# Row order of the second spectrum stage: loads that write 128 partitions instead of 64

## Chip, cores and metric

The kernel runs on one core of one Trainium2 chip. The metric is the device time of one execution in microseconds; several runs give a median and the spread. A profiled execution gives the trace from which the views come: engines PE (TensorE matmul), PEld (its weight load), DVE (VectorE), ACT (ScalarE), POOL (GpSimd) and SP (SyncE, which here issues nearly all DMAs).

## What is computed

One block with two branches, each behind a layer norm with a learned scale and shift: a diagonal state-space convolution along the 2048 tokens, then a token-mixing MLP. The convolution is written with FFTs of length 4096 over 448 channels:

```python
h = _layernorm(x, axis=-1) * (1 + ca) + sa
x = x + ga * _A_ref(h, A_log_A_real, A_A_imag, A_C_real, A_C_imag, A_log_dt, A_D_skip)
h = _layernorm(x, axis=-1) * (1 + cb) + sb
x = x + gb * _B_ref(h, B_w1, B_b1, B_w2, B_b2)
...
# in _A_ref
K = 2.0 * jnp.einsum("dn,dnl->dl", C, P).real
Kf = jnp.fft.rfft(K, L2)
Uf = jnp.fft.rfft(u_t, L2)
y = jnp.fft.irfft(Uf * Kf[None, :, :], L2)[:, :, :L]
```

## The kernel before

The kernel computes the FFTs as two stages of matmuls against tables of cosines and sines. 4096 points are split in 64 x 64; the first stage (`n1` to `k1`) handles 32 tokens at a time, the second (`n2` to `k2`) contracts 128 rows: 64 values of `n2` times the two parts `c` (real, imaginary).

The spectrum of the input u goes as follows. `u_rows` (lines 537 to 558) does the first stage: for each group R and g it makes a tile `yt` and stores it with SP into the DRAM tensor `yu_d`, of shape `[o, k, c, R, g, d]` = `[2, 32, 2, 8, 4, 448]` (line 553). The letters o, R and g together number the 64 values of `n2` (n2 = 16 g + 2 R + o), k is the 32 columns `k1`, c the part, d the channel. `u_load(n)` (lines 567 to 571) loads columns 2n and 2n+1 back: a tile `yi` of 128 partitions x 2 columns x 448 channels, in two DMAs. `u_cols(k)` (lines 573 to 600) does the second stage of column k: one matmul `pu` (line 580) of `yi[:, k % 2]` with the table tile `s2`, whose rows must stand in the same order as those of `yi`. ACT (line 589) or DVE (line 587) evicts `pu` to `uo`, and SP stores each pair of columns into `us_d` (line 593). After both columns of pair n, `u_load(n + 4)` reuses the buffer (there are four), and every second pair `s2_load` (line 565) fetches another part of the table `S2`.

The same stretch of the program also makes the convolution's own kernel, in 56 steps s: exponents and phases by matmul (line 627; `halves`, called by `st_exponents` and `st_phase`) from small tables `lex` and `lph`, which SP loads from the DRAM tensors `pars` (lines 613 and 617, upper and lower rows); exp and sin on ACT (lines 650, 683 to 688); products on DVE and POOL (lines 690 to 696); `kg` on PE (line 717). `lex` has four buffers and `lph` three, so a load waits for PE to have read the table four or three groups earlier. `chain(q)` makes the parameters on DVE and POOL and stores them into `pars` (line 396).

Steps 16 to 31 interleave this with `u_cols`: two or three columns a step, and one after each exponential of the window at step 24. At step 32 the pools of this stage close, and the next stage loads `us_d` as `u` (line 782) and the inverse tables `si` (line 789).

The order on PE, ACT, DVE and POOL is written out by hand (a manual schedule). SP's order is left to a scheduler from step 8 on; it places each DMA by when it expects it to be ready. SP issues in its order and waits for what the next DMA needs: the producer's or the last reader's semaphore, and the DMA eight places earlier, since completions are counted on eight semaphores in turn.

Of the kernel before, what the change touches and what calls it, by code (L numbers as in the profile page):

```python
# [22 lines left out]
P = 128  # L23
# [18 lines left out]
def dft_tables():  # L42
    n1 = np.arange(32)
    k1 = np.arange(32)
    n2 = np.arange(64)
    k2 = np.arange(64)
    nn = 4096
    t = {}
    w = 2 * np.pi * np.outer(n1, k1) / 64
    w1 = np.zeros((2, 32, 32))  # L50
    w1[0] = np.cos(w)
    w1[1] = -np.sin(w)
    w1[0, :, 0] = 1
    w1[1, :, 0] = (-1.0) ** n1
    wc = np.zeros((4, 32, 2, 4, 32))
    for g in range(4):
        for c in range(2):
            wc[g, :, c, g, :] = w1[c]
    t["WU"] = np.tile(w1.transpose(1, 2, 0).reshape(32, 64), (4, 1))

    t["WC"] = wc.reshape(P, 2, 2, 2, 32).swapaxes(3, 4).reshape(P, 2 * P)
    s = np.zeros((2, 64, 32, 2, 64))
    i1 = np.zeros((2, 64, 32, 2, 64))
    i2 = np.zeros((2, 64, 32, 2, 64))

    def inverse(rows, cols, k, m, ang):
        a = np.cos(ang) * 2 / nn
        b = np.sin(ang) * 2 / nn
        i1[0, rows, k, m[0]] = a
        i1[1, rows, k, m[0]] = -b  # L70
        i2[1, rows, k, m[0]] = -a
        i2[0, rows, k, m[0]] = -b
        if len(m) > 1:
            i1[0, rows, k, m[1]] = b
            i1[1, rows, k, m[1]] = a
            i2[1, rows, k, m[1]] = -b
            i2[0, rows, k, m[1]] = a

    for k in range(1, 32):
        ang = 2 * np.pi * np.outer(n2, k + 64 * k2) / nn  # L80
        s[0, :, k, 0] = np.cos(ang)
        s[1, :, k, 0] = np.sin(ang)
        s[0, :, k, 1] = -np.sin(ang)
        s[1, :, k, 1] = np.cos(ang)
        inverse(slice(None), None, k, (0, 1), ang.T)


    for q in range(32):
        ang = 2 * np.pi * n2 * (32 + 64 * q) / nn
        s[1, :, 0, 0, q] = np.cos(ang)  # L90
        s[1, :, 0, 1, q] = -np.sin(ang)
        inverse(q, None, 0, (1,), ang)
    for q in range(33, 64):
        ang = 2 * np.pi * n2 * (64 * (q - 32)) / nn
        s[0, :, 0, 0, q] = np.cos(ang)
        s[0, :, 0, 1, q] = -np.sin(ang)
        inverse(q, None, 0, (0,), ang)
    s[0, :, 0, 0, 32] = 1
    s[0, :, 0, 1, 32] = (-1.0) ** n2
    i1[0, 32, 0, 0] = 1 / nn  # L100
    i2[1, 32, 0, 0] = (-1.0) ** n2 / nn
    s2 = s.reshape(P, 32 * P)

    t["S2"] = s.reshape(2, 4, 8, 2, 32 * P).transpose(3, 0, 2, 1, 4).reshape(P, 32 * P)

    one = np.einsum("cnk,cqkm->km", w1, s.reshape(2, 64, 32, P))
    t["SV"] = one[ones_k1()].T

    order = lambda a: a.reshape(P, 32, 2, 2, 2, 16).transpose(0, 1, 5, 2, 4, 3)
    t["I1"] = order(i1)  # L110
    t["I2"] = order(i2)
    ft = np.zeros((32, 2, 2, 32, 2))
    w = 2 * np.pi * np.outer(k1, n1) / 64
    f0 = np.cos(w)
    f1 = -np.sin(w)
    f0[0] = 1
    f1[0] = (-1.0) ** n1
    for h in range(2):
        ft[:, 0, h, :, h] = f0
        ft[:, 1, h, :, h] = f1  # L120
    t["FT"] = ft.reshape(P, 64)
    fl = np.zeros((4, 4, 2, 2, 2 * LAST, 2, 64))
    for r in range(2):
        for g in range(2):
            fl[r, :, g, r, :, g] = t["FT"].reshape(32, 4, 64)[-2 * LAST :].swapaxes(0, 1)
    t["FL"] = fl.reshape(32, 2 * 2 * LAST * P)


    te = np.zeros((3, 64, 16, 32))
    tg = np.zeros((3, 16, 4, 16, 32))  # L130
    n = np.arange(32)
    for d in range(16):
        te[0, 2 * d : 2 * d + 2, d] = 2 * n + 1
        te[2, 2 * d : 2 * d + 2, d] = -n
        tg[0, d, 0:2, d] = 128 * n
        tg[0, d, 2:4, d] = 1
        tg[2, d, 0:2, d] = -64 * n
        tg[2, d, 2:4, d] = 1
    tg = tg.reshape(3, 16, 2, 2, 512).swapaxes(1, 2)
    tt = np.concatenate([te.reshape(3, 64, 512), tg.reshape(3, 64, 512)], 1)  # L140
    tt[1] = -tt[0]
    t["TT"] = tt.reshape(3, P, 512)

    v1, v2 = (t.pop(k).reshape(2, 64, 32, P) for k in ("I1", "I2"))
    j1 = np.stack([v1[0], v2[1]])
    j2 = np.stack([v1[1], v2[0]])
    for nm, tabs, n in (("SI", (s2, v1, v2), NP), ("SJ", (s2, j1, j2), 1), ("SK", (s2, v1), NP)):
        tabs = [a.reshape(P, NP, 2, P)[:, :n] for a in tabs]  # L150
        t[nm] = np.stack(tabs, 2).reshape(P, n * len(tabs) * 2 * P)
    return {k: np.ascontiguousarray(v.astype(np.float32)) for k, v in t.items()}


def ones_k1():

    return [0] + list(range(1, 32, 2))
# [69 lines left out]
def tile_adaln_s4d_mixer(ctx, tc, i, out):  # L227
    nc = tc.nc
# [5 lines left out]
    yu_d = dram.tile([2, 32, 2, 8, 4, D], F32, name="yu_d")  # L234
# [13 lines left out]
    with ExitStack() as es:  # L248
# [309 lines left out]
            dve.append(out)  # L558

        yis, s2s, uos = {}, {}, {}  # L560
        yu_v = yu_d.rearrange("o k c R g d -> o (c R g) k d")

        def s2_load(n):
            s2s[n] = sp2.tile([P, 4, P], F32, tag="s2", name="s2")
# [2 lines left out]
        def u_load(n):  # L567

            yis[n] = up.tile([P, 2, D], F32, tag="yi", name="yi", bufs=4)
            for o in range(2):  # L570
                nc.sync.dma_start(yis[n][64 * o : 64 * o + 64], yu_v[o, :, 2 * n : 2 * n + 2])

        def u_cols(k):
            n, kk = divmod(k, 4)
            if kk % 2 == 0:
                uos[k // 2] = up.tile([P, 2, 2, DC], F32, tag="uo", name="uo", bufs=4), []
            yi, s2 = yis[k // 2], s2s[n]
            uo, done = uos[k // 2]
            pm = pms.tile([P, D], F32, tag="ms", name="pu")
            T.matmul(pm, s2[:, kk], yi[:, k % 2], start=True, stop=True)  # L580

            def out():
                o, chunks = uo[:, :, k % 2], lambda t: t.rearrange("p (c d) -> p c d", c=2)
                if k in ones_k1():

                    j = ones_k1().index(k)
                    stt(o, chunks(mod[0]), svt[:, j : j + 1], chunks(pm), ALU.mult, ALU.add)
                else:
                    S.copy(o, chunks(pm))
                done.append(kk)  # L590
                if len(done) == 2:
                    to = us_d[:, :, k // 2 * 2 : k // 2 * 2 + 2].rearrange("c p k d -> p c (k d)")
                    nc.sync.dma_start(to, uo.rearrange("p c k d -> p c (k d)"))

            (dve if k in ones_k1() else act).append(out)
            if k % 2 and k // 2 + 4 < 16:
                u_load(k // 2 + 4)
                if kk == 3 and n + 2 < 8:
                    s2_load(n + 2)
# [481 lines left out]
        for s in range(tail):  # L1081
# [68 lines left out]
            if s == 16:  # L1150
                spec.close()
                up = early.enter_context(tc.tile_pool(name="up", bufs=2))
                for n in range(4):
                    u_load(n)
# [49 lines left out]
        for k in range(NP + 1):  # L1204

            n = NP + k
# [46 lines left out]
    with ExitStack() as es:  # L1253
# [165 lines left out]
        for t in range(16):  # L1419
# [3 lines left out]
            o = pacc.tile([P, D], F32, tag="acc", name="o")  # L1423
            for kh in range(2):
                n = 32 + 2 * t + kh
# [38 lines left out]
```

## Time and profile before

| | us |
|---|---|
| runs | 692.27, 692.97, 697.21 |
| median | 692.97 |
| the profiled execution | 694.13 |
| its span | 692.3 |
| `yi` loads issued (32 of 224 KB) | from 139.3 to 195.3 |
| `pu` matmuls that read them | from 145.6 to 208.9 |
| first `u` load of the next stage | 218.48 |

The span is the time from the first to the last instruction of the profiled execution; 694.13 - 692.3 = 1.8 us lie around it. Positions in the trace count from the span's start. The page's timeline has 40 slices of 17.3 us; digits are tenths of busy time. A row of a stretch gives its length, the busy us of each engine with the count of instructions, the granted clock of TensorE, the mean share of the 16 DMA engines and GB/s. The share can come out a little over 1 where packets overlap.

### The profile page before, as it was taken

How to read it: one execution, taken by the hardware profiler on the slowest of the kernel's cores; microseconds unless marked ns; L12 is line 12 of the kernel's file. 1: busy time of each engine (PE TensorE's matmuls, PEld its weight loads, DVE VectorE, ACT ScalarE, POOL GpSimd, SP SyncE). 2: the span in 40 equal slices, each digit the busy share in tenths (PEclk: the TensorE clock that was granted, in tenths of full speed). 3: DMA queues.
4: the chain of work that ended last, by engine and by line, in shares of the span. 5: the costliest groups of instructions: out<-in, count | busy, mean ns of one | idle time of the engine just before them, and what ended most of it. 6: DMA issues, size and time to landing. Idle time of an engine off the chain costs nothing.

```text
span 692.3 us, 18523 instructions
## 1 busy us (share of the span) xinstructions
PE 640.5 (93%) x7322; PEld 485.1 (70%) x7322; DVE 428.3 (62%) x818; ACT 451.4 (65%) x848; POOL 278.2 (40%) x367
## 2 busy tenths in 40 slices
PE   0867999999988899999999979999999999999997
PEld 0434454455445676676789757778899999999997
DVE  7887789787576584856745567776732364444431
ACT  5877598899889899999767668787322352222220
POOL 6694569578488767777568100000000000000000
PEclk9998999999999999999999999999999999999999
DMA  7595647589795586554589799965674445555640
GB/s 184 178 200 142 211 159 247 207 223 290 204 280 160 139 169 168 142 158 128 153 257 378 238 259 235 240 148 143 185 218 109 145 133 160 160 164 169 164 128 27
DMA packets 99438, 128.14 MB, mean 185 GB/s; under 512 B 13460, under 2 KB 79928, under 8 KB 99352
## 3 DMA queue, kind: packets, MB, share of 16 engines
q1 hardware_dynamic: 98152, 123.42, 63.3%
q0 software_dynamic: 1200, 3.54, 2.2%
q8 instruction: 58, 0.95, 0.6%
q14 instruction: 28, 0.23, 0.1%
HBM read 91.57 MB, written 34.87 MB: 183 GB/s over the span
## 4 chain that ended last, share of the span: by engine, by line
PE 70%; ACT 12%; DVE 5%; DMA 5%; issue 4%; POOL 2%; SPq 2%; DVEq 0%; ACTq 0%; POOLq 0%
PE o L1432 7%; PE xe L627 6%; PE o L1431 6%; PE o L1430 6%; PE acc L1271 6%; PE acc L1272 6%; PE acc L1273 6%; PE kg L717 5%; PE vv L836 3%; PE kx L820 3%; PE vv L837 3%; PE pu L548 3%; PE pu L580 2%; ACT mag L650 2%; PE xg L627 2%
## 5 line engine op out<-in xcount | busy, mean ns | idle before, releaser
L212 ACT CAST whi<-w 128x896 fp32r<-128x896 f32 x64 | 59.8, 940 | 133.0 <-PE o L1431 81.2
L221 DVE TENSOR_TENSOR wlo<-w,whi 128x896 fp32r<-128x896 f32 x64 | 68.1, 1086 | 38.9 <-ACT whi L212 35.8
L690 POOL TENSOR_TENSOR G<-mag,gs 128x512 f32<-128x512 f32 x56 | 71.9, 1284 | 49.4 <-ACT gs L686 49.4
L1271 PE MATMUL acc<-h3h,whi 128*128 128x448 f32 x224 | 83.4, 372 | 1.7 <-ACT h3h L1338 0.9
L1272 PE MATMUL acc<-h3l,whi 128*128 128x448 f32 x224 | 82.1, 367 | 1.1 <-DVE h3l L1345 0.9
L1273 PE MATMUL acc<-h3h,wlo 128*128 128x448 f32 x224 | 81.7, 365 | 0.0
L1432 PE MATMUL o<-uh,wlo 128*128 128x448 f32 x224 | 81.3, 363 | 0.0
L1431 PE MATMUL o<-ul,whi 128*128 128x448 f32 x224 | 81.2, 362 | 0.0
L1430 PE MATMUL o<-uh,whi 128*128 128x448 f32 x224 | 80.6, 360 | 0.0
L717 PEld LDWEIGHTS kg<-E,G 128*32 128x32 f32 x3584 | 54.5, 111 | 31.4 <-issue 21.2
L691 POOL TENSOR_TENSOR G<-mag,gs 128x512 f32<-128x512 f32 x56 | 71.8, 1282 | 0.0
L717 PE MATMUL kg<-E,G 128*32 128x64 f32 x3584 | 64.1, 223 | 6.1 <-issue 5.5
L627 PE MATMUL xg<-tab,lph 64*128 64x512 f32 x112 | 61.3, 547 | 7.4 <-DVE E L696 3.2
L627 PE MATMUL xe<-tab,lph 64*128 64x512 f32 x112 | 61.3, 547 | 1.1 <-ACT gs L687 0.9
L692 DVE TENSOR_TENSOR E<-m,xe 128x512 f32<-128x512 f32 x53 | 36.3, 686 | 40.9 <-ACT xe L685 20.3
L1435 DVE TENSOR_TENSOR y<-o,x 128x448 f32<-128x448 f32 x16 | 10.0, 625 | 79.0 <-PE o L1432 79.0
L671 POOL TENSOR_TENSOR m<-mag,w 128x512 f32<-128x512 f32 x53 | 55.6, 1048 | 4.2
L1271 PEld LDWEIGHTS acc<-h3h,whi 128*128 128x128 f32 x224 | 42.4, 189 | 15.1 <-ACT h L1343 4.2
L1272 PEld LDWEIGHTS acc<-h3l,whi 128*128 128x128 f32 x224 | 42.5, 190 | 4.3 <-DVE h3l L1345 1.2
L828 DVE TENSOR_TENSOR z<-kx,u 128x448 f32<-128x448 f32 x48 | 28.4, 620 | 26.4 <-PE kx L820 26.4
L1273 PEld LDWEIGHTS acc<-h3h,wlo 128*128 128x128 f32 x224 | 42.4, 189 | 2.8
L1431 PEld LDWEIGHTS o<-ul,whi 128*128 128x128 f32 x224 | 42.0, 188 | 3.2
(246 smaller groups left out, 1508.4 us busy)
## 6 DMA issues: line engine op xcount, KB each, us to landing
w<-in_B_w_dram SPq DMA_DIRECT2D x64, 224.0 KB
w<-in_B_w_dram SPq DMA_DIRECT2D x32, 448.0 KB
yu_d<-yt SPq DMA_DIRECT2D x16, 448.0 KB
yi<-yu_d SPq DMA_DIRECT2D x32, 224.0 KB
us_d<-uo SPq DMA_DIRECT2D x16, 448.0 KB
u<-us_d SPq DMA_DIRECT2D x32, 224.0 KB
v_d<-vt SPq DMA_DIRECT2D x32, 224.0 KB
vt<-v_d SPq DMA_DIRECT2D x14, 448.0 KB
```

The costliest lines, as they stand in the source:

```text
L212: self.nc.scalar.copy(hi, w)
L221: eng.tensor_tensor(lo, w, hi.bitcast(F32), ALU.subtract)
L627: T.matmul(out[k], lhs[r], rhs[r], start=start, stop=stop)
L690: G.tensor_tensor(Gt[:, 1], mg_, v32(sg), ALU.mult)
L691: G.tensor_tensor(Gt[:, 0], mg_, v32(cg_), ALU.mult)
L717: T.matmul(kg[32 * q : 32 * q + 32, m], Gt[:, c, d], E[:, c, d], start=h == 0 and c == 0 and m == 0, stop=h == 1 and c == 1, skip_group_ch ...
L1271: nc.tensor.matmul(acc[f], hi[:, fs], h3h[:, r], start=r == 0, stop=False)
L1272: nc.tensor.matmul(acc[f], hi[:, fs], h3l[:, r], start=False, stop=False)
L1273: nc.tensor.matmul(acc[f], lo[:, fs], h3h[:, r], start=False, stop=r == 15)
L1430: nc.tensor.matmul(o, hi[:, ks], uh[kh][:, k], start=kh == 0 and k == 0, stop=False)
L1431: nc.tensor.matmul(o, hi[:, ks], ul[kh][:, k], start=False, stop=False)
L1432: nc.tensor.matmul(o, lo[:, ks], uh[kh][:, k], start=False, stop=kh == 1 and k == 6)
```

## The change

The rows of the second stage are numbered (c, R, g, o) instead of (o, c, R, g). The table `S2`, made on the host, is permuted alike, so the products are the same and only the order of summation over partitions differs. `u_load` still issues two DMAs of 224 KB, each of 128 rows of 1792 bytes. Before, one DMA filled 64 partitions (one value of o) with both columns; now one DMA fills all 128 partitions with one column, and reads in turn from o = 0 and o = 1.

```diff
-    t["S2"] = s.reshape(2, 4, 8, 2, 32 * P).transpose(3, 0, 2, 1, 4).reshape(P, 32 * P)
+    t["S2"] = s.reshape(2, 4, 8, 2, 32 * P).transpose(0, 2, 1, 3, 4).reshape(P, 32 * P)
...
-        yu_v = yu_d.rearrange("o k c R g d -> o (c R g) k d")
+        yu_v = yu_d.rearrange("o k c R g d -> k (c R g) o d")
...
             yis[n] = up.tile([P, 2, D], F32, tag="yi", name="yi", bufs=4)
-            for o in range(2):
-                nc.sync.dma_start(yis[n][64 * o : 64 * o + 64], yu_v[o, :, 2 * n : 2 * n + 2])
+            for k in range(2):
+                nc.sync.dma_start(yis[n][:, k], yu_v[2 * n + k])
```

A matmul of column k now needs one of the two DMAs where it needed both. The order of instructions on PE, DVE, ACT and POOL is unchanged. On SP, the scheduler places other DMAs differently between step 16 and step 32. In the rows below a name such as `lph_144<-pars_58` is a table tile and the parameter tensor that it is loaded from; `yi<-yu_d` is the changed load.

Place one, the first loads of the stage on SP, before:

```order
L617 DMA lex_148<-pars_58 64x1x256
L571 DMA yi<-yu_d 64x2x448 x10
L613 DMA lph_144<-pars_58 32x256
L617 DMA lph_144<-pars_58 64x1x256
L593 DMA us_d<-uo 128x2x448
L571 DMA yi<-yu_d 64x2x448 x2
```

and now:

```order
L617 DMA lex_148<-pars_58 64x1x256
L571 DMA yi<-yu_d 128x1x448 x8
L613 DMA lph_144<-pars_58 32x256
L617 DMA lph_144<-pars_58 64x1x256
L571 DMA yi<-yu_d 128x1x448 x2
L613 DMA lph_142<-pars_58 32x256
L593 DMA us_d<-uo 128x2x448
L571 DMA yi<-yu_d 128x1x448 x2
```

The load of `lph_144` is now ahead of the pair of `yi` loads that waits for the first columns, and half of `lph_142` ahead of the first `us_d` store.

Place two, on SP at the window of step 24, where the parameters' last stores begin, before:

```order
L593 DMA us_d<-uo 128x2x448
L613 DMA lph_144<-pars_58 32x256
L617 DMA lph_144<-pars_58 64x1x256
L396 DMA pars_60<-hl 128x1x128 x6
L571 DMA yi<-yu_d 64x2x448 x2
```

and now:

```order
L593 DMA us_d<-uo 128x2x448
L613 DMA lex_145<-pars_59 32x256
L617 DMA lex_145<-pars_59 64x1x256
L396 DMA pars_60<-hl 128x1x128 x6
L571 DMA yi<-yu_d 128x1x448 x2
```

The exponents' table `lex_145` of a later group stands where `lph_144` stood; `lph_144` has gone further up, ahead of the `yi` and `S2` loads that precede this store.

Place three, the end of the stage on SP, before:

```order
L593 DMA us_d<-uo 128x2x448 x3
L613 DMA lph_143<-pars_59 32x256
L617 DMA lph_143<-pars_59 64x1x256
L613 DMA lex_145<-pars_59 32x256
L617 DMA lex_145<-pars_59 64x1x256
L613 DMA lex_146<-pars_59 32x256
L617 DMA lex_146<-pars_59 64x1x256
L613 DMA lex_147<-pars_59 32x256
L617 DMA lex_147<-pars_59 64x1x256
L613 DMA lex_148<-pars_59 32x256
L617 DMA lex_148<-pars_59 64x1x256
L593 DMA us_d<-uo 128x2x448 x2
```

and now:

```order
L593 DMA us_d<-uo 128x2x448
L613 DMA lph_143<-pars_59 32x256
L617 DMA lph_143<-pars_59 64x1x256
L613 DMA lex_147<-pars_59 32x256
L617 DMA lex_147<-pars_59 64x1x256
L613 DMA lex_148<-pars_59 32x256
L617 DMA lex_148<-pars_59 64x1x256
L593 DMA us_d<-uo 128x2x448 x3
L613 DMA lph_144<-pars_59 32x256
L617 DMA lph_144<-pars_59 64x1x256
L593 DMA us_d<-uo 128x2x448
```

Two of the four `lex` tables have gone earlier; the six loads that stay are ahead of the last four `us_d` stores instead of the last two.

## Prediction

> **What bounds the kernel now.** I began with the page: share of each engine, then the 40 slices, then the chain that ended last.
>
> ```profile
> span 692.3 us, 18523 instructions
> PE 640.5 (93%) x7322; PEld 485.1 (70%) x7322; DVE 428.3 (62%) x818; ACT 451.4 (65%) x848; POOL 278.2 (40%) x367
> ...
> PE   0867999999988899999999979999999999999997
> ...
> DMA  7595647589795586554589799965674445555640
> ...
> PE 70%; ACT 12%; DVE 5%; DMA 5%; issue 4%; POOL 2%; SPq 2%; DVEq 0%; ACTq 0%; POOLq 0%
> ```
>
> TensorE is the bound (93% busy, 70% of the chain). A slice is 17.3 us; the changed loads are issued from 139 to 196 us, slices 8 to 11, where PE shows 9 9 9 8 and the DMA engines are busy too. So the next question was which of the two sets the pace there. I asked for everything that touches the tile `yi`, then for busy time by stretch.
>
> ```profile
> L580 PEld LDWEIGHTS pu<-yi,s x64: 186/189/190, 145.6 to 208.5; 128*128 128x128 f32 x64
> L580 PE MATMUL pu<-yi,s x64: 539/539/643, 145.6 to 208.9; 128*128 128x448 f32 x64
> L571 SPq DMA_DIRECT2D yi<-yu_d x32: 573/605/1167, 139.3 to 195.3; - x32
> its engine sat idle before it (us, times) until:
>   issue: 7.4, 32
>   DVE E L693: 3.7, 2
>   ACT uo L589: 2.0, 4
>   DVE uo L587: 0.8, 2
>   DMA us_d<-uo: 0.3, 1
> ```
>
> The list of releasers has no `DMA yi<-yu_d` in it: not one of the 64 matmuls that read the tile was seen waiting for the tile's loads. ("issue" is idle time of the weight loader, 0.23 us each, which is not PE idle.)
>
> ```profile
> 139.00:212.00 73.00, 68.51 (x1129) 36.75 (x1127) 52.51 (x99) 66.30 (x132) 53.90 (x66) 1.00 0.85 243
> 212.00:235.00 23.00, 19.24 (x452) 12.71 (x452) 12.16 (x21) 22.69 (x43) 20.45 (x28) 1.00 0.67 176
> 142.00:148.00 6.00, 4.75 (x72) 2.61 (x73) 4.74 (x8) 5.97 (x13) 5.78 (x6) 1.00 1.08 237
> 196.00:199.00 3.00, 2.88 (x74) 1.73 (x74) 1.57 (x3) 0.80 (x2) 2.92 (x4) 1.00 1.05 361
> 220.00:226.00 6.00, 5.67 (x173) 3.71 (x177) 0.56 (x1) 6.00 (x14) 5.36 (x10) 1.00 1.00 249
> 363.00:381.00 18.00, 18.00 (x97) 18.00 (x96) 9.40 (x16) 13.00 (x24) 14.47 (x28) 1.00 1.05 375
> ```
>
> After the stretch stand its length, busy us of PE, PEld, DVE, ACT, POOL, then clock, DMA share and GB/s. In the stage of the loads (139 to 212) PE is busy 68.51 of 73.00 us: all its idle time is 4.5 us. The clock is full. Row three is the best measure of the old loads: from 142 to 148 the queue holds almost nothing but them, all 16 engines are full (1.08), and they move 237 GB/s. Rows four and six are full engines with mostly 128-partition transfers: 361 and 375 GB/s.
>
> **The change, part by part.**
>
> *The loads themselves.* There are 32 before and after, 224 KB each, in 1792-byte rows. With full engines an old one occupies them 229,376 B / 237 GB/s = 0.97 us. For the new one no row exists; the bounds are 0.97 us (no gain) and 0.61 us (375 GB/s). I take 0.63 us (361 GB/s), the rate of the nearest row in time, in which stores of the same row size run over 128 partitions. So the 16 engines are freed for 32 x (0.97 - 0.63) = 11 us within the stage. On the path this is worth 0 unless somebody waits for the loads. To see how far from that it is, I set issue times of SP against the matmuls that use each load.
>
> ```profile
> 139.33 9.26 SPq L571 DMA_DIRECT2D yi<-yu_d  x10
> ...
> 151.21 1.56 SPq L571 DMA_DIRECT2D yi<-yu_d  x2
> ...
> 169.01 0.37 SPq L593 DMA_DIRECT2D us_d<-uo  x1
> ...
> 187.10 1.26 SPq L571 DMA_DIRECT2D yi<-yu_d  x2
> ...
> 198.28 5.63 SPq L593 DMA_DIRECT2D us_d<-uo  x3
> ```
>
> ```profile
> 145.56 1.77 PE L580 MATMUL pu<-yi,s 128*128 128x448 f32 x4
> ...
> 164.79 1.77 PE L580 MATMUL pu<-yi,s 128*128 128x448 f32 x4
> ...
> 169.73 0.49 PE L627 MATMUL xg<-tab,lex 64*128 64x512 f32 x1
> ...
> 171.81 0.42 PE L717 MATMUL kg<-E,G 128*32 128x64 f32 x13 [0.68 <-issue]
> ...
> 196.12 0.99 PE L580 MATMUL pu<-yi,s 128*128 128x448 f32 x2 [1.50 <-DVE E L693]
> ...
> 198.67 0.58 PE L627 MATMUL xg<-tab,lph 64*128 64x512 f32 x1
> ```
>
> The tile has four buffers, so loads run four pairs ahead. Pair 0: issued at 139.33, used at 145.56, 6.2 us later. Pair 5: 151.21 and 164.79, 13.6 us. Pair 12, the closest of the later ones: 187.10 and 196.12, 9.0 us, and there PE waits for VectorE, not for data. The last row of idle time in this list that I cannot put down to an engine is the 0.68 us of "issue" at 171; with the 0.3 us on a `us_d` store that is 1.0 us that lighter DMA traffic might return. Bounds for this term: -1.0 and 0; I take -0.2, close to the end that has the 32 readings on its side.
>
> *One load per matmul instead of two.* Column k now needs only its own load. That moves a wait that is never the last: 0. The cover is the 6 to 13 us of lead above.
>
> *Issue time on SP.* An old issue takes 605 ns at the median. A 128-partition `us_d` store takes 0.37 us; so 32 x (0.61 - 0.37) = 8 us at most come free on SP, or none. SP spends the stage waiting for what it is to move, not issuing:
>
> ```profile
> SPq L593 <- DVE uo L587: 7.7, 7, 4.3
> SPq L571 <- PE pu L580: 5.4, 6, 2.1
> ...
> SPq L571 <- DMA yi<-yu_d: 0.9, 2, 0.7
> SPq L593 <- DMA yi<-yu_d: 0.6, 2, 0.3
> ```
>
> (total us, times, longest). So 0 on the path. Only about 2 us of SP's waits are for an earlier `yi` load to leave its slot, and these go.
>
> *The order on SP.* The rows on PE, DVE, ACT and POOL are in the same order as before; on SP the table loads `lph` and `lex` move. A moved load holds everything behind it until PE has read the old contents. Place two: `lex_145` is now ahead of the `pars` stores, right after the store at 169.01, so SP reaches it at 169.4; PE's last read of the old table is the matmul of 169.73 + 0.49 = 170.2: SP is held 0.8 us. Place three: `lph_143` now stands behind the first of the three `us_d` stores of 198.28, and PE frees it at 198.67 + 0.58 = 199.25: under 1 us. Then six loads of some 0.5 us are ahead of two `us_d` stores, which come up to 3 us later. Who needs those? The first `u` loads of the next stage, which wait for the last store anyhow:
>
> ```profile
> 211.41 0.68 DVE L587 SCALAR_TENSOR_TENSOR uo<-mod,svt,pu 128x448 f32<-128x448 f32 x1
> ...
> 219.28 1.28 DVE L761 COPY yk<-y 128x512 f32<-128x512 f32 x2
> ```
>
> ```profile
> 209.92 2.60 SPq L593 DMA_DIRECT2D us_d<-uo  x2
> ...
> 218.48 1.26 SPq L782 DMA_DIRECT2D u<-us_d  x2
> ```
>
> VectorE makes the last `uo` at 211.41 + 0.68 = 212.1, so the last store goes out then in either order. Bounds of the order's term: 0 and +3 us; I take 0.
>
> *The permuted table.* Same size, same loads, same matmuls: 0.
>
> Sum: -0.2 + 0 + 0 + 0 + 0 = -0.2 us. The profiled execution took 694.13 us with a span of 692.3; its span becomes 692.1. It stands 1.2 us above the median of the runs, 692.97, so the forecast is 692.97 - 0.2 = 692.8 us.
>
> **The rivals.**
>
> *The stage was held by the full DMA engines without showing it (faster).* For it: shares of 1.08. Against it: PE is busy 68.51 of 73.00 us. If every idle microsecond of PE from 139 to 212 went, the time would be 692.97 - 4.5 = 688.5; with those of 212 to 235 (23.00 - 19.24 = 3.8) 684.7.
>
> *SP held by the moved table loads (slightly slower).* If the 3 us reached PE: 696.0. Against it: `yk` at 219.28 and the `u` loads at 218.48 hang on the last store, which doesn't move. It decides only where the last store comes later than 212.1.
>
> *The new loads read two distant places and become slow (slower).* A new load fetches, for each of 64 rows, one from o = 0 and one from o = 1, which lie 32 x 2 x 8 x 4 x 448 x 4 B = 3,670,016 B apart; the old one read one side only. Free DMA time in the stage is 15% of 73 us = 11 us, or 0.34 us a load: it decides from 0.97 + 0.34 = 1.31 us a load. At half of row three's rate (1.94 us a load, an assumed size, since no row shows one) the engines need 32 x 0.97 = 31 us more, 11 of which are free: 692.97 + 20 = 713. Against it: the `u` loads read two halves of `us_d` that lie 128 x 32 x 224 x 4 B = the same 3,670,016 B apart, and with them the engines move 249 GB/s at a share of 1.00 (220 to 226). [...]
>
> *The loads get no faster.* If reading DRAM rather than writing partitions sets 237 GB/s, nothing is freed: 693.0, the same within what can be measured. The Trainium skill (SBUF — State Buffer, Door 1) says that 64 partitions reach only 8 of 16 ports, 218 GB/s at most, which makes this less likely; no run here separates the two yet.
>
> **How the numbers follow.** Forecast 0.82 (692.8); hidden DMA bound 0.06 (688.5 or less); SP held 0.05 (696.0); no faster 0.03 (693.0); distant reads 0.04 (713). About 1%, 7 us, is what a measurement of this kernel can tell from no change. Faster by more than that is the tail of the first rival, where idle time beyond 212 us goes too: 0.03. Slower: the distant reads with 0.01 of the held queue: 0.05. Within 1%: 0.92. The range takes the forecast's terms (-1.0 to +3 us on 692.97) and, below, half of the first rival's way: 690.5 to 696.0.
>
> **What would show it.** Right: no matmul of line 580 waits for `yi`; the stretch 142 to 148 moves well over 300 GB/s or has a share well under 1; the DMA share of 139 to 212 falls from 0.85 to about 0.70 while PE's busy time there stays near 68.5 us; the last `us_d` store near 212 us. Wrong: `DMA yi<-yu_d` among the releasers of line 580; the first `u` load well after 218.5 us; a share that stays at 0.85; or PE's 4.5 us of idle time in the stage halved.

## The result and the profile after

The changed kernel takes 697.88 us (median of 13 runs, 694.34 to 703.3) beside 694.02 us (median of 13 runs, 691.75 to 697.21) of the kernel before in the same rounds. The ratio is 1.0051, with a 95% interval of 1.003 to 1.0072: about 3.5 us slower. (A ratio is estimated over the runs of both kernels in the same rounds; it need not equal the quotient of the two medians, here 697.88 / 694.02 = 1.0056.) The forecast was 692.8 us, within 690.5 to 696.0. Of the 5.1 us between forecast and measurement 1.05 us is the kernel before itself, whose median over 13 runs is 694.02 where the forecast started from 692.97. The profiled execution took 695.99 us. I read the profile after in the order of the one before. First the page: span, busy shares, the row of DMA shares in 40 slices, and the chain's shares.

```profile
span 694.2 us, 18542 instructions
PE 641.3 (92%) x7322; PEld 484.7 (70%) x7322; DVE 428.4 (62%) x818; ACT 450.1 (65%) x848; POOL 278.9 (40%) x367
...
DMA  7594647578775466463579899985573445555540
...
PE 69%; ACT 12%; DVE 6%; DMA 6%; issue 4%; POOL 2%; SPq 1%; DVEq 0%; POOLq 0%; ACTq 0%
```

The slices 8 to 11 of the loads (counted from 0) went from 8 9 7 9 to 7 8 7 7: lighter. TensorE is as busy as before. The stretches (length, busy us of PE, PEld, DVE, ACT, POOL, then clock, DMA share, GB/s):

```profile
139.00:212.00 73.00, 67.18 (x1081) 35.97 (x1083) 50.19 (x92) 63.39 (x125) 52.41 (x64) 0.98 0.76 244
142.00:148.00 6.00, 4.74 (x81) 2.63 (x82) 4.51 (x8) 5.97 (x13) 5.84 (x8) 1.00 0.76 246
196.00:199.00 3.00, 2.00 (x14) 0.74 (x18) 0.84 (x2) 0.14 (x1) 2.57 (x4) 0.61 1.04 398
196.60:200.00 3.40, 3.00 (x50) 1.74 (x54) 0.24 (x1) 0.53 (x1) 1.97 (x3) 0.51 1.05 403
```

From 142 to 148 the engines move as much as before (246 GB/s beside 237) at a share of 0.76 instead of 1.08: the new loads occupy them less. But from 196.6 to 200.0 TensorE has half its clock, where the kernel before had 1.00. What the tile `yi` shows (instructions, then idle time by releaser):

```profile
L580 PE MATMUL pu<-yi,s x64: 539/539/1085, 144.8 to 211.1; 128*128 128x448 f32 x64
L571 SPq DMA_DIRECT2D yi<-yu_d x32: 513/598/1240, 138.8 to 196.0; - x32
its engine sat idle before it (us, times) until:
  issue: 7.8, 33
  DVE E L696: 6.9, 2
  ACT uo L589: 2.0, 4
```

Again no matmul waits for `yi`. The second releaser was "DVE E L693: 3.7, 2" and is now "DVE E L696: 6.9, 2" (matmul and weight load counted apart). That row led to the place. TensorE's rows there (start, length, count, and in brackets the idle time ahead), first before:

```profile
192.85 1.77 PE L580 MATMUL pu<-yi,s 128*128 128x448 f32 x4 [0.23 <-ACT uo L589]
...
197.04 1.10 PE L717 MATMUL kg<-E,G 128*32 128x64 f32 x64
...
212.07 1.10 PE L717 MATMUL kg<-E,G 128*32 128x64 f32 x64 [0.54 <-POOL G L690]
```

and after:

```profile
192.13 1.77 PE L580 MATMUL pu<-yi,s 128*128 128x448 f32 x4 [0.24 <-ACT uo L589]
197.00 1.83 PE L580 MATMUL pu<-yi,s 128*128 128x448 f32 x2 [3.10 <-DVE E L696]
198.76 1.69 PE L717 MATMUL kg<-E,G 128*32 128x64 f32 x64
...
214.37 1.10 PE L717 MATMUL kg<-E,G 128*32 128x64 f32 x64 [0.54 <-POOL G L690]
```

At 192 the changed kernel is 192.85 - 192.13 = 0.72 us ahead; at 212 it is 214.37 - 212.07 = 2.30 us behind. It loses 3.0 us at one place: the idle time ahead of column 24 is 3.10 us instead of the 1.50 us that the prediction quoted (1.6 us), and the next matmuls run at half speed (1.83 for 0.99, 1.69 for 1.10: 1.4 us). (Every column is two matmul records, so x2 is column 24 alone.) After that the difference wanders, and the span ends 1.9 us longer. The mean granted clock is 0.988 in both profiled executions, since each has half-clock slots at other places too (before, for example, from 235.0 to 238.4 and from 409.1 to 412.5). So this pair of profiles shows where the changed kernel loses time, but not what the clock costs in all.

What does column 24 wait for? The releaser named, `E`, is no operand: line 580 reads `yi` and `s2` alone, and only the matmuls of line 717 read `E`. Column 24 is the first of a new part of the table `S2`. SP's rows, before:

```profile
188.46 0.54 SPq L593 DMA_DIRECT2D us_d<-uo  x1
189.09 1.53 SPq L571 DMA_DIRECT2D yi<-yu_d  x2
190.67 0.60 SPq L565 DMA_DIRECT2D s<-in_S_dram  x1
```

and after:

```profile
187.71 0.54 SPq L593 DMA_DIRECT2D us_d<-uo  x1
188.30 0.46 SPq L613 DMA_DIRECT2D lex<-pars  x1
188.81 0.53 SPq L617 DMA_DIRECT2D lex<-pars  x1
189.44 0.38 SPq L613 DMA_DIRECT2D lph<-pars  x1
189.92 0.52 SPq L617 DMA_DIRECT2D lph<-pars  x1
190.53 1.21 SPq L571 DMA_DIRECT2D yi<-yu_d  x2
191.79 0.58 SPq L565 DMA_DIRECT2D s<-in_S_dram  x1
```

Four table loads (`lex_146`, `lph_142`) are now ahead of the S2 load, which is issued at 191.79 instead of 190.67, though the kernel was 0.72 us ahead. Column 24 follows 5.45 us after the issue before (190.67 to 196.12) and 5.21 us after it now. The semaphore updates kept in the traces settle what it waited for: the last update of this S2 load comes at 196.03 before and at 196.91 now, each 0.09 us ahead of column 24. That holds in all ten profiles of kernels that load the table in eight parts (0.05 to 0.14 us ahead), also where the page names VectorE or "issue". So the 1.50 us that the prediction quoted was a wait for the table as well.

### The profile page after: what moved, and what is told of

Same layout as the page of the kernel before. It is cut to its first block, busy times and chain, and to the rows that moved or that the text cites. A ratio compares the mean times of both kernels' runs of the same rounds, so it can differ in the third digit from the quotient of the medians.

```text
span 694.2 us, 18542 instructions
## 1 busy us (share of the span) xinstructions
PE 641.3 (92%) x7322; PEld 484.7 (70%) x7322; DVE 428.4 (62%) x818; ACT 450.1 (65%) x848; POOL 278.9 (40%) x367
## 3 DMA queue, kind: packets, MB, share of 16 engines
q0 software_dynamic: 1200, 3.54, 2.2%
## 4 chain that ended last, share of the span: by engine, by line
PE 69%; ACT 12%; DVE 6%; DMA 6%; issue 4%; POOL 2%; SPq 1%; DVEq 0%; POOLq 0%; ACTq 0%
PE o L1431 7%; PE o L1430 6%; PE o L1432 6%; PE xe L627 6%; PE acc L1271 6%; PE acc L1272 6%; PE acc L1273 5%; PE kg L717 5%; PE vv L836 3%; PE vv L837 3%; PE kx L820 3%; DMA w<-in_B_w_dram 3%; ACT mag L650 2%; PE pu L548 2%; PE pu L580 2%
## 5 line engine op out<-in xcount | busy, mean ns | idle before, releaser
L1430 PEld LDWEIGHTS o<-uh,whi 128*128 128x128 f32 x224 | 42.1, 188 | 3.3
```

The lines of the kernel that those rows point to most:

```text
L1430: nc.tensor.matmul(o, hi[:, ks], uh[kh][:, k], start=kh == 0 and k == 0, stop=False)
```

## Experiments

**Theory T:** the four loads delay the S2 load, TensorE waits longer for it, and the longer idle time is followed by half clock; the shape of the loads costs nothing. **R1:** the shape costs the time. **R2:** half-clock slots and stray waits that have nothing to do with the order.

Five kernels use a function that adds order edges on SP (no semaphore, no wait) before step 32, along a list of instruction names, so that SP's order can be chosen apart from the loads:

```diff
+            if s == 32: fix_order(tc, nc)
...
+def fix_order(tc, nc):
+    made = {i.name: i for i in nc.cur_bb.bb.instructions}
+    info = mybir.DependencyInfo(mybir.DependencyClass.NoSync, mybir.DependencyReason.DATA)
+    for a, b in ORDER:
+        tc.add_manual_dep(made[b], a, info, reason="issue order")
```

### shape_only: new loads, old order

Edit: the changed kernel, with the list of the kernel before.

> The changed loads and the permuted table, with SP's order of the kernel before (from step 16 to step 32, forced by added order edges; no wait and no instruction is added). Theory T (the four table loads that now stand ahead of the S2 load of columns 24 to 27 make TensorE wait 3.1 instead of 1.5 us for column 24, and the longer idle time is followed by 3.4 us at half clock): this kernel loses both, so its ratio to the kernel before is 0.997 to 1.001, column 24's idle time is at most 1.5 us, and no half-clock slot follows it. Rival R1 (the shape of the loads costs the time: reads from two distant places, or bursts that delay others): ratio 1.004 to 1.007, as the changed kernel. Rival R2 (half-clock slots and stray issue waits that fall anywhere, whatever the order): ratio 1.000 to 1.005 with half-clock slots at other places.

Measured: 692.05 us, ratio 0.9962 (0.9932 to 0.9992). TensorE, then SP:

```profile
192.45 1.77 PE L580 MATMUL pu<-yi,s 128*128 128x448 f32 x4 [0.24 <-ACT uo L589]
194.88 0.99 PE L580 MATMUL pu<-yi,s 128*128 128x448 f32 x2 [0.65 <-DVE E L696]
195.80 1.10 PE L717 MATMUL kg<-E,G 128*32 128x64 f32 x64
```

```profile
189.92 0.61 SPq L565 DMA_DIRECT2D s<-in_S_dram  x1
```

As T says, and a little better than its range (0.997 to 1.001): column 24 waits 0.65 us and the matmuls run at full speed. R1 falls: the new shape alone makes the kernel faster, by 0.4% (0.1 to 0.7%). The S2 load is issued earlier (189.92) and used 4.96 us later, where it took 5.45 us with the old loads ahead of it.

### order_only: old loads, new order

Edit: the kernel before, with the list of the changed kernel.

> The old loads and the old table, with SP's order of the changed kernel (steps 16 to 32, forced). T: column 24 waits about 3 us and a half-clock slot follows; ratio to the kernel before 1.003 to 1.008 (the old loads take more DMA time, so the S2 load may land still later). R1: ratio 0.999 to 1.001 and column 24 near 1.5 us. R2: anything from 1.000 to 1.005 with no tie to column 24.

Measured: 698.39 us, ratio 1.0061 (1.0029 to 1.0094). TensorE:

```profile
191.41 1.77 PE L580 MATMUL pu<-yi,s 128*128 128x448 f32 x4 [0.24 <-ACT uo L589]
198.51 1.83 PE L580 MATMUL pu<-yi,s 128*128 128x448 f32 x2 [5.34 <-issue]
```

The stretch that follows (the clock is the third number from the end):

```profile
197.50:204.00 6.50, 5.49 (x74) 2.99 (x74) 0.00 (x0) 0.53 (x1) 0.41 (x1) 0.50 0.88 290
```

The order alone costs what the whole change costs. With the old loads ahead of it the S2 load, issued at 191.40, is used 7.1 us later, and the wait is 5.34 us, where T had about 3: the order is the loss, and the new shape softens it.

### s2_first: one move back

Edit: the changed kernel's list with three names (two `yi` loads and the S2 load) moved ahead of four. The lines below name the loads in place of the list's instruction numbers.

```diff
-lex_146 (L613, L617), lph_142 (L613, L617), yi (L571, two), S2 (L565)
+yi (L571, two), S2 (L565), lex_146 (L613, L617), lph_142 (L613, L617)
```

> The changed kernel with one move: on SP the loads of yi for pair 14 and the S2 load of columns 24 to 27 go ahead of the four table loads (lex_146, lph_142) that the scheduler had put before them; all the rest of SP's order as in the changed kernel. T: column 24's idle time is back at 1.5 us or less, no half-clock slot there, ratio to the kernel before 0.998 to 1.001. R1: 1.004 to 1.007, since the loads are as in the changed kernel. A second form of the order theory (the later tables, or the us_d stores at the end of the stage, cost the time, not the S2 load): 1.003 to 1.007 with column 24 at 1.5 us.

Measured: 693.48 us, ratio 0.9976 (0.9946 to 1.0006). TensorE:

```profile
194.30 0.99 PE L580 MATMUL pu<-yi,s 128*128 128x448 f32 x2 [0.57 <-DVE E L696]
...
202.67 0.61 PE L580 MATMUL pu<-yi,s 128*128 128x448 f32 x1 [0.66 <-DMA s<-in_S_dram]
```

One move takes the loss away, with all the other moves of the order kept; the ratio is just under T's range (0.998 to 1.001). The second row is column 28, the next part of the table, and here the profile does name the table's load.

### tables_ahead: the four loads alone

Edit: the list of shape_only with the four table loads moved up to where the changed kernel has them, and nothing else.

> The kernel of shape_only (changed loads, SP's order of the kernel before) with one move: the four table loads lex_146 and lph_142 ahead of the yi loads of pair 14 and the S2 load of columns 24 to 27, as the changed kernel has them. T: the S2 load is issued some 1.9 us later than in shape_only, column 24 waits 2.3 to 3.3 us where shape_only showed 0.65, and where that passes about 3 us a half-clock slot follows; ratio to the kernel before 1.000 to 1.006, that is 0.3 to 1 per cent above shape_only's 0.9962. If the cost of the order lies in its other moves (the end of the stage, place three): 0.995 to 0.999.

Measured: 696.67 us, ratio 1.0042 (1.0016 to 1.0068). TensorE, then the clock of the slot behind it:

```profile
197.49 0.99 PE L580 MATMUL pu<-yi,s 128*128 128x448 f32 x2 [3.54 <-DMA s<-in_S_dram]
198.41 1.69 PE L717 MATMUL kg<-E,G 128*32 128x64 f32 x64
```

```profile
198.70:202.00 3.30, 3.30 (x68) 1.95 (x56) 0.00 (x0) 0.35 (x1) 0.00 (x1) 0.51 1.01 353
```

The four loads alone make the loss. The wait (3.54 us) is a little over the range expected, and this time its releaser is named rightly: the load of `s`.

### s2_halves: the wait taken out of the program

Edit: the changed kernel, with the table in 16 loads of two columns and four buffers, asked for eight columns ahead.

```diff
-            s2s[n] = sp2.tile([P, 4, P], F32, tag="s2", name="s2")
-            nc.sync.dma_start(s2s[n], s2_v[:, 4 * n : 4 * n + 4])
+            s2s[n] = sp2.tile([P, 2, P], F32, tag="s2", name="s2", bufs=4)
+            nc.sync.dma_start(s2s[n], s2_v[:, 2 * n : 2 * n + 2])
...
-                if kk == 3 and n + 2 < 8:
-                    s2_load(n + 2)
+                s2_load(k // 2 + 4)
```

> The changed kernel with the S2 table in 16 loads of two columns (128 KB) in four buffers of half the size, same memory; the load for a pair of columns is asked for eight columns ahead, where the old form asked for the table of column 24 after column 19. SP's order is the scheduler's own. T: the wait for the table at columns 24 (3.1 us in the changed kernel, 1.5 in the one before) goes altogether, so 1.5 us are won on the kernel before and the half-clock slot does not come: ratio to the kernel before 0.995 to 0.999. R1: 1.003 to 1.007. R2: no tie, about 1.000 to 1.005.

Measured: 692.39 us, ratio 0.9952 (0.992 to 0.9984). TensorE:

```profile
194.02 2.52 PE L580 MATMUL pu<-yi,s 128*128 128x448 f32 x6 [0.24 <-ACT uo L589]
196.47 1.10 PE L717 MATMUL kg<-E,G 128*32 128x64 f32 x64
```

The group of six matmuls is columns 22 to 24, two matmuls each: column 24 does not wait at all. As T expected. This version is faster than both kernels and needs no fixed order (SP's order is another one again, the scheduler's own); it can't be told from shape_only (0.9962), whose interval overlaps.

### halves_old: the same with the old loads

Edit: s2_halves with the old `yi` loads and the old table, SP's order fixed to that of s2_halves.

> The kernel with the S2 table in 16 loads, but with the old yi loads and the old table, and SP's order of s2_halves forced up to step 32. Column 24's wait for the table is gone in both, so what differs is the shape of the loads alone. T (the shape acts on the time only through the S2 load's landing): ratio to the kernel before 0.995 to 0.999, the same as s2_halves (0.9952) within the intervals. If the shape is worth something by itself (11 us of DMA time freed): 0.999 to 1.002, slower than s2_halves, with yi or other loads among what TensorE waits for. If the new shape costs: below 0.994.

Measured: 693.06 us, ratio 0.9996 (0.9969 to 1.0022). T's range (0.995 to 0.999) missed it; the second case of the expectation held, and the load that TensorE waits for is again the table and not `yi`. The row is column 26, the first of the next part of the table:

```profile
200.18 1.74 PE L580 MATMUL pu<-yi,s 128*128 128x448 f32 x4 [1.15 <-DMA s<-in_S_dram]
```

With the old loads this part of the table comes late even when asked for earlier: its last semaphore update follows 6.00 us after the issue (194.05 to 200.05), beside 4.57 us in s2_halves (194.29 to 198.86). That the shape is worth something through what stands behind the loads is what the two profiles show; the ratios (0.9996 and 0.9952) have intervals that overlap, and alone they do not settle it.

### after_again, fill24, fill24_few, before_again: the clock

Edits: the changed kernel once more; the changed kernel with the gap ahead of column 24 filled in two ways; the kernel before once more.

```diff
# fill24
-            yi, s2 = yis[k // 2], s2s[n]
+            yi, s2 = (k == 24 and warm(20), yis[k // 2])[1], s2s[n]
# fill24_few
+            for _ in range(5 * (k == 24)): T.matmul(pm, tab[0:64, 1, 0:P], tab[0:64, 1, 0:D], start=True, stop=True)
             T.matmul(pm, s2[:, kk], yi[:, k % 2], start=True, stop=True)
```

> The changed kernel, unedited, once more beside the others. T and every rival that puts the cost down to the change: ratio 1.003 to 1.007, and in its profile column 24 waits near 3 us with a half-clock slot behind it. If the slot and the ratio came from stray disturbances of one execution, this profile has no slot at column 24, or the ratio is near 1.000.

> The changed kernel with 20 spare matmuls (ones times ones, 128x256, about 0.11 us each, 2.2 us in all, added to the half of the kg tile that the kernel's own fillers use, products that are not read) put on TensorE ahead of column 24's matmul, where it now waits 3.1 us. SP's order ahead of the S2 load is as in the changed kernel, so the wait's end stays where it was. T with the clock as a second part: the idle time left is about 1 us, no half-clock slot follows, column 24 starts no later than before, and 1.5 us of the 3 us come back: ratio to the kernel before 1.000 to 1.004. If idle time of TensorE has nothing to do with the half-clock slot, the slot stays and the ratio is 1.003 to 1.008.

> The changed kernel with the gap ahead of column 24 filled by 5 spare matmuls on 64 rows of a table already in SBUF (128x448, about 0.4 us each, into the accumulator that column 24 then overwrites): the same fill as fill24 with 5 instructions instead of 20, so that TensorE's instruction stream is shifted little. T with the clock as a part of it: no half-clock slot at column 24, and ratio 0.999 to 1.005. If fill24's stall of 3.58 us at 222.9 us came from the fill itself and not from the shift of the instruction stream, it comes again and the ratio is 1.006 to 1.011. If idle time is no cause of the half-clock slot, the slot stays at column 24.

> The kernel before, unedited, profiled once more. T: column 24 waits 1.2 to 1.8 us and no half-clock slot follows it; between 205 and 245 us, where the profiles of all the other kernels lost 1 to 5 us on the first profile of the kernel before, this one loses some of that too if the loss there is a matter of the single execution.

Measured: after_again 698.7 us, ratio 1.0071 (1.0041 to 1.01), idle 3.32 us at column 24 and 6.8 us of half clock around it, as T expected. fill24 699.36 us (six runs), 1.0085 (1.0051 to 1.0119); fill24_few 696.73 us, 1.0018 (0.9987 to 1.0048); before_again a single execution, 694.06 us. TensorE of fill24:

```profile
192.84 2.35 PE L639 MATMUL kg<-ones 128*128 128x256 bf16 x20
196.15 0.99 PE L580 MATMUL pu<-yi,s 128*128 128x448 f32 x2 [0.96 <-DVE E L696]
...
226.49 0.58 PE L627 MATMUL xg<-tab,lex 64*128 64x512 f32 x1 [3.58 <-issue]
```

of fill24_few, with the slot behind its column 24:

```profile
196.62 1.29 PE L579 MATMUL pu<-tab 64*128 64x448 f32 x5
199.69 1.02 PE L580 MATMUL pu<-yi,s 128*128 128x448 f32 x2 [1.78 <-DMA s<-in_S_dram]
```

```profile
200.90:204.30 3.40, 3.40 (x68) 2.05 (x57) 0.00 (x0) 0.37 (x1) 0.53 (x1) 0.50 1.04 371
```

and of before_again:

```profile
195.28 0.99 PE L580 MATMUL pu<-yi,s 128*128 128x448 f32 x2 [1.43 <-DVE E L693]
```

In fill24 the fill does at column 24 what T expected: 0.96 us of idle time, full clock. Its time is nevertheless as bad as the changed kernel's, and its profile shows another loss: 3.58 us at 222.9, which is no wait that the profile knows. So its time decides nothing between the two cases of its expectation. In fill24_few the fill was too short (1.29 us), 1.78 us of idle time stayed, and so did the slot; the 3.58 us did not come again, but the interval is too wide to put a price on the clock. In before_again column 24 is as in the first profile; and as expected of a matter of the single execution, it loses 1.5 us on that one between 219 and 224 (0.86 us ahead at one matmul, 0.62 us behind at a later one). That loss is a half-clock slot from 219.0 to 222.4, and the longest idle time of TensorE just ahead of it is 0.66 us.

What twelve profiles say together of column 24: where it waits 0 (s2_halves, halves_old), 0.57, 0.65, 0.96, 1.43 or 1.50 us, no half clock follows; where it waits 1.78, 3.10, 3.32, 3.54 or 5.34 us, half clock sets in during the wait or up to 1.2 us after it, for 3.4 or 6.8 us. At this place the order of those numbers leaves R2 little room. Elsewhere R2 holds: every profile has half-clock slots at other places, and the limit between 1.50 and 1.78 us is not a general one. In the profile before, 1.83 us of idle time at 35.2 was followed by none, and a slot began at 235.0 after idle times of 0.89 and 0.97 us (at 232.6 and 234.0).

The mean granted clock over all runs is 0.983 for the changed kernel (13 runs) and for after_again (12), 0.987 for the kernel before, 0.988 to 0.989 in shape_only, s2_first, s2_halves and halves_old, 0.984 in tables_ahead and 0.986 in the two fills. That goes with the slot at column 24, but other slots are in it too. And order_only does not fit: its mean is 0.987, no lower than that of the kernel before, though its one profile (701.18 us, clock 0.983) has 6.8 us of half clock there. Its longer wait alone (5.34 - 1.50 = 3.8 us) is near its loss of 0.0061 x 694 = 4.2 us.

## Why the prediction was wrong, point by point

**The order on SP was the step that failed.** Its term was 0, with bounds 0 and +3 us. I costed two places, the `pars` stores and the end of the stage. At neither did the moved loads cost anything that the runs show: s2_first keeps both and gives 0.9976. The text of the change even said that two `lex` tables "have gone earlier", and I costed what they leave, not what they now stand ahead of. They stand ahead of the S2 load. With the new loads the order costs (1.0051 - 0.9962) x 694 = 6.2 us, and its four table loads alone (1.0042 - 0.9962) x 694 = 5.6 us; with the old loads it costs 4.2 us. Each is beyond the bound of +3 us. The loads' own gain pays part of it back, and what is left beside the kernel before is, in the one profile, 1.6 us of wait and 1.4 us of half clock. Over all runs the lower clock is a time at half speed of 2 x (0.987 - 0.983) x 697 = 5.6 us more, which costs half, 2.8 us, as long as TensorE is busy: with the wait 4.4 us, beside the measured 3.5 us (0.0051 x 694) and 4.9 us (0.0071 x 694). The wait is shown; the clock's part of the sum is an estimate, since no run took the slot away and left the wait.

**A row was misread.** I quoted "[1.50 <-DVE E L693]" and wrote that PE waits for VectorE there, not for data. VectorE's `E` is no operand of that matmul. The wait was for the table, whose load landed 0.09 us ahead of it, so the place had no cover at all. Against the program the S2 load went out 1.84 us later (1.12 us, while TensorE was 0.72 us ahead), and 1.60 us of that reached TensorE. I had looked for waits on `yi`, the tile that the change names, and not on the other operand of the same matmul, which comes through the same queue.

**The rival "SP held by the moved table loads" was right in kind (696.0 us, chance 0.05), and its place was wrong.** It was to decide only where the last `us_d` store comes later than 212.1. That store goes out at 214.44 now, so the condition came true, but it is 2.3 us later as everything is by then, and the first `u` load at 217.34, earlier than the 218.48 before. Nothing was lost there.

**The loads themselves: direction right, size off.** I took 0.34 us less of DMA time a load, 11 us in all, and a share of about 0.70 from 139 to 212. The share fell from 0.85 to 0.76: 0.09 x 73 = 6.6 us, 0.21 us a load. Its worth on the path was put at -0.2 us; shape_only measures 0.0038 x 694 = 2.6 us (0.6 to 4.7). The same wait is part of it: with lighter engines the S2 load lands sooner, and column 24 waits 0.65 us instead of 1.50. Those 0.85 us lie within the measured interval; no profile shows where the rest would come from. So a case of the hidden-bound rival held in part: a load did hold TensorE, though not the one that I searched.

**Distant reads** fell: the loads that alternate between two places move 246 GB/s at a share of 0.76. The Trainium skill (DMA: Bandwidth & Descriptors, Latency and other measured facts) has copies slowed at row pitches of large powers of two. The 3,670,016 B here are 3.5 MiB, which is not one, and only two places alternate, so no run here tests that rule. **Loads get no faster** fell by the same row: a share of 0.76 beside 1.08 at nearly the same GB/s. That 64 partitions are the slower target, as the Trainium skill has it (SBUF — State Buffer, Door 1), agrees with this trace. Its 218 GB/s is for one set of 64 partitions; the 237 GB/s of the old loads are more, with loads to both halves on the queue. The order of the reads changed along with the partitions, so no run here separates the two.

**One load per matmul, SP's issue time and the permuted table** were put at 0 and show nothing: no wait for `yi`, and an issue takes 598 ns at the median beside 605.

**Of what should show it,** the stretch 142 to 148 (share well under 1), PE's busy time near 68.5 us (67.18; 69.09 in shape_only) and no wait for `yi` came true, and said nothing of the loss, which lay in a row that I had taken for VectorE's. One sign failed: the last `us_d` store near 212 us came at 214.44.

**Still open:** what part of the loss is the half clock's alone, since fill24 lost its gain elsewhere and fill24_few's interval is wide. Why the scheduler ranks the four loads earlier was not tried.

## What to carry to other kernels

Where a scheduler places the DMAs, a change of a transfer's shape is also a change of the queue's order, and the order can be worth more than the shape (here +0.6% beside -0.4%). Before costing a moved load at nothing, list what stands behind it on its queue and check every operand of the consumer, not only the tile that the change names. A releaser that neither makes an operand of the waiting instruction nor frees its output buffer is not what it waited for; look for the operand whose load is the latest.

## What the runs showed of the hardware that was not expected

- At column 24 TensorE's clock fell to half around a short idle time in an otherwise busy stretch: in twelve profiles never with 1.50 us or less, always with 1.78 us or more, for 3.4 or 6.8 us. Elsewhere in the same profiles that limit does not hold (no slot after 1.83 us at 35.2 in before, one after 0.89 and 0.97 us at 235.0). In the changed kernel's profile a wait of 1.6 us more thus went with a loss of 3.0 us at this place.
- A 256 KB load took about 5 us from issue to use while the DMA engines' share was 0.89 to 1.06 (4.8 to 5.6 us with the new loads ahead of it, 5.45 to 7.1 us with the old).
- TensorE can stop for 0.9 to 3.6 us with nothing named. The changed kernel shows it inside a run of 64 matmuls:

```profile
227.77 0.44 PE L755 MATMUL y<-wc,ks 64*64 64x64 f32 x11
229.34 1.03 PE L755 MATMUL y<-wc,ks 64*64 64x64 f32 x53 [1.12 <-issue]
```

  s2_first stops at the same matmul of the run (0.90 us, before its last 53), and fill24, with 20 more matmuls and their weight loads ahead, stops 18 matmuls earlier (the 3.58 us). The other nine profiles show no such stop there, and after_again, the same program as the changed kernel, is one of them. The instruction queue's packets (q8, 16 KB each) fit: the three stops end 1.3 to 1.5 us after such a packet landed (228.0, 224.3 and 225.0), and in the nine the packet landed 1.6 to 3.9 us ahead of the same matmul. That points to the fetching of instructions, which no experiment tried.
